# Turning x of one chunk by a transfer on ScalarE's queue, and a new order in six passes of a fused attention and max-FFN kernel

## The chip, the core and the metric

One core of one Trainium2 chip. Five engines work side by side, each with its own stream of instructions: TensorE (PE, with weight loads shown apart as PEld), VectorE (DVE), ScalarE (ACT), GpSimd (POOL) and SyncE (SP), which here only starts transfers. Transfers started by SP, ACT or POOL stand in that engine's queue and are carried out by the core's 16 DMA engines. The metric is the device time of one execution in microseconds (us), the median of several runs.

## What is computed

A sliding-window attention with sink positions, then a feed-forward layer whose hidden value is the maximum of three products. Batch 4, 8 heads, 768 positions, head size 64; a position sees the first 4 positions and the 128 up to itself.

```python
scores = scale * np.matmul(q, k.transpose(0, 1, 3, 2))
keep = is_sink | in_window              # pos < 4, or 0 <= rel < 128
scores = np.where(keep, scores, -1000000000.0)
a = softmax(scores)                     # over the last axis
attn = np.matmul(a, v)                  # (4, 8, 768, 64)
x = attn.transpose(0, 2, 1, 3).reshape(3072, 512)
h = np.maximum(np.maximum(x @ w1, x @ w2), x @ w3)   # 512 -> 768
return (h @ w_out).astype(np.float32)                # 768 -> 512
```

## The kernel before, in words

The 3072 positions are cut into 12 chunks of 256 (`NCH = 12`, three per batch entry, `CPB = 3`). For one chunk the steps are:

- `load(ci)` (L90, SP's queue): k, q and v of the chunk, 512 KB each, into raw tiles; two raw tiles of each kind exist. `cast(ci)` (L101, L105, POOL in the loop) makes bf16 of them.
- `turn_dma(ci, 'k')` and `turn_dma(ci, 'q')` (L159 in two halves, L154): transposing transfers on SP's queue that write kT and qT, of which a ring of four exists. The first chunks are turned by TensorE instead.
- `sink_score` (L300) and `score(ci, pairs)` (L274): TensorE, 64 rows of the array per head, two heads to a pair, four pairs; a pair's scores fill two PSUM banks. A chunk that opens a batch entry has no sink step, and its scores have three blocks instead of four. `sink_k` and `sink_v` (L230, L316) prepare the sinks of a batch entry, once for each.
- `expo` (L286, ACT; L306 for the sinks), which frees the two banks of a pair, and `mask` (L292, DVE).
- `av_open` (four banks, and the sink products L332, 32 rows of the array each) and `av(ci, pair)` (L350 on TensorE, then L355 and L358 on DVE, which write a pair's part of x).
- x turned into xT: `xpose(ci, t)` does it on TensorE (L371, four matmuls against an identity for each half, then a copy out of PSUM, L372), `xpose_dma(ci)` by one transposing transfer on SP's queue (L377). Chunks 0 to 3 use `xpose`, chunks 4 to 11 `xpose_dma`. Three xT tiles exist.
- `ffn_h(ci, fp, wi)` (L390): eight matmuls of the chunk's xT with 256 columns of weight matrix `wi`; with `wi = 0` ACT copies the result to h (L397), with 1 or 2 DVE takes the maximum (L401). Nine calls make the chunk's h.
- `ffn_y(ci, t)` (L411): six matmuls of 512 columns, then a copy out of PSUM (L413), and `store(ci)` (L427, SP's queue).

The order is written out by hand: every engine carries out its instructions in the order in which the calls stand. PSUM's eight banks are given out by a list: `bank` takes the one at its front, and the step that empties a bank puts it at the back, so the order of the calls decides which bank each step takes and whose end it waits for. Chunks 0 to 2 and the attention of chunk 3 stand in a long straight part; then a loop runs over `i = 3 .. 11`. A pass of the loop has, interleaved, the loads of chunk `i + 3`, the casts and turns of chunk `i + 2`, the attention of chunk `n = i + 1`, the first layer of chunk `i` and the second layer of chunk `m = i - 1`.

In a pass before, SP's queue gets the three loads, k in two halves, q, the store of `m` and x of `n`, in this order. TensorE gets the sink scores, pairs 0 and 1, `ffn_y(m, 0)`, pairs 2 and 3, `ffn_y(m, 1)`, two `ffn_h`, and then the four `av` between further `ffn_h`. Both copies of y are on DVE.

Of the kernel before, what the change touches and what calls it, by code (L numbers as in the profile page):

```python
# [16 lines left out]
def kernel(  # L17
# [31 lines left out]
    with tc.manual_schedule():  # L49
# [26 lines left out]
        def load(ci, what="kqv", gate=None, part=None, parts=1):  # L76
            if ci >= NCH:
                return
            b, c = divmod(ci, CPB)
            t0 = c * 256  # L80
            for w in what:
                src = {"k": k, "q": q, "v": v}[w]
                if (ci, w) not in raws:
                    raws[ci, w] = raw.tile([128, H, 2, D], F32, tag=w + "_raw", name=w + "_raw")
                dst = raws[ci, w]
                if gate is not None:
                    gate(dst[0:1, 0, 0, 0:1])
                n = H // parts
                for g in range(parts) if part is None else (part,):
                    nc.sync.dma_start(  # L90
                        out=dst[:, n * g:n * g + n],
                        in_=src[b, n * g:n * g + n, t0:t0 + 256]
                            .rearrange("h (p i) d -> p h (i d)", i=2))
# [56 lines left out]
        def turn_dma(ci, w):  # L150
            if ci >= NCH:
                return
            if w == "q":
                nc.sync.dma_start_transpose(  # L154
                    out=qT[ci % RING].rearrange("q p i n r -> q (p i) (n r)"),
                    in_=bfs[ci, w].rearrange("s p i a d -> s (p i a d)"))
                return
            for n in range(2):
                nc.sync.dma_start_transpose(  # L159
                    out=kT[ci % RING][:, n].rearrange("q p i r -> q (p i) r"),  # L160
                    in_=bfs[ci, w][64 * n:64 * n + 64].rearrange("q p i a d -> q (p i a d)"))
# [64 lines left out]
        def sink_k(b):  # L226
            x = kT[(b * CPB) % RING]
            for a in range(2):
                hp = slice(64 * a, 64 * a + 64)
                nc.gpsimd.tensor_copy(  # L230
                    ks[b % 2][hp, :, 4 * a:4 * a + 4].rearrange("q p (r i) -> q p r i", i=2),
                    x[hp, 0, :, :, 0:2].rearrange("q p i r -> q p r i"))
# [77 lines left out]
        def sink_v(b):  # L310

            x = vb[(b * CPB) % RING]
            sv = bank([128, 2, D + 1], F32, "sv")
            for a in range(2):
                for p in range(NP):
                    nc.tensor.matmul(  # L316
                        sv[32 * p:32 * p + 32, a], lhsT=sel[:, a], rhs=x[:, 0, 2 * p + a],
                        start=True, stop=True, tile_position=(0, 32 * p))
            nc.vector.tensor_copy(vs[b % 2], sv)
            give(sv)  # L320
# [18 lines left out]
        def av(ci, p):  # L339
            b, c = divmod(ci, CPB)  # L340
            o = os_[ci, p]
            e = es[ci, p][0]
            first = c == 0
            for t in range(2):
                for a in range(2):
                    blocks = [(1, ci, 0)] if t == 0 else [(2, ci, 0), (3, ci, 1)]
                    if t == 0 and c:
                        blocks = [(0, ci - 1, 1)] + blocks
                    for s, cv, n in blocks:
                        nc.tensor.matmul(  # L350
                            o[:, t, a], lhsT=e[:, a, s], rhs=vb[cv % RING][:, n, 2 * p + a],
                            start=first, stop=True, skip_group_check=True)
                        first = False
            rc = work.tile([128, 2, 2], F32, tag="rc", bufs=4, name="rc")
            nc.vector.reciprocal(rc, o[:, :, :, D])  # L355
            if p == 0:
                xs[ci] = work.tile([128, 2, NP, 2, D], BF16, tag="x", bufs=2, name="x_sb")
            nc.vector.tensor_mul(xs[ci][:, :, p], o[:, :, :, 0:D],  # L358
                                 rc.unsqueeze(3).to_broadcast([128, 2, 2, D]))
            give(o)  # L360
# [3 lines left out]
        def xpose(ci, t, eng=None):  # L364
            eng = eng or nc.scalar
            if t == 0:
                xTs[ci] = work.tile([128, 2, DS, 128], BF16, tag="xT", bufs=3, name="xT")
            pt = bank([128, DS, 128], BF16, "xt")
            x = xs[ci][:, t].rearrange("q p a d -> q (p a d)")
            for ds in range(DS):  # L370
                nc.tensor.transpose(pt[:, ds], x[:, ds * 128:(ds + 1) * 128], ident)  # L371
            (nc.scalar.copy if eng is nc.scalar else eng.tensor_copy)(xTs[ci][:, t], pt)  # L372
            give(pt)

        def xpose_dma(ci):
            xTs[ci] = work.tile([128, 2, DS, 128], BF16, tag="xT", bufs=3, name="xT")
            nc.sync.dma_start_transpose(  # L377
                out=xTs[ci].rearrange("q t s r -> q (t s) r"),
                in_=xs[ci].rearrange("q t p a d -> q (t p a d)"))

# [2 lines left out]
        def ffn_h(ci, fp, wi, cuts=1):  # L383
            if ci not in hs:
                hs[ci] = work.tile([128, FB, 256], BF16, tag="h", bufs=3, name="h_sb")
            hp = bank([128, 2, 256], F32, "h_ps")
            for f in range(2):
                c0 = (2 * fp + f) * 128
                for ds in range(DS):
                    nc.tensor.matmul(  # L390
                        hp[:, f].rearrange("q (i t r) -> q i t r", i=2, t=2),
                        lhsT=w_sb[wi][:, ds, c0:c0 + 128],
                        rhs=xTs[ci][:, :, ds].rearrange("q t (i r) -> q i t r", i=2),
                        start=(ds == 0), stop=(ds == DS - 1))
            dst = hs[ci][:, 2 * fp:2 * fp + 2]
            if wi == 0:
                nc.scalar.copy(dst, hp)  # L397
            else:
                for f in range(cuts):
                    x = slice(2 * f // cuts, 2 * (f + 1) // cuts)  # L400
                    nc.vector.tensor_max(dst[:, x], dst[:, x], hp[:, x])  # L401
            give(hp)
# [40 lines left out]
        def cast(ci, q=None):  # L443
            if ci >= NCH:
                return
            for w in "kq":
                for g in range(2):
                    cast_qk(ci, w, g, q if q and w == "q" else nc.gpsimd)
            for n in range(2):
                for i in range(2):  # L450
                    cast_v(ci, n, i, nc.gpsimd)
# [195 lines left out]
        ffn_h(2, 2, 2)  # L647
        av(3, 3)
        av(3, 2)
        ffn_h(2, 1, 1)  # L650
        ffn_h(2, 1, 2)
        load(5, 'v', gate=after(0))
        xpose(3, 0, nc.scalar)
        xpose(3, 1, nc.vector)
        ffn_h(2, 2, 1)
        for i in range(3, NCH):
            n, m = i + 1, i - 1
            more = n < NCH
            if more:
                n % CPB == 1 and (sink_k(n // CPB), sink_v(n // CPB))  # L660
            load(i + 3)
            cast(i + 2)
            turn_dma(i + 2, 'k')
            turn_dma(i + 2, 'q')
            if more:
                sink_score(n)
            if more:
                score(n, (0, 1))
            if more:
                expo(n, 0)  # L670
            if more:
                expo(n, 1)
            ffn_y(m, 0, nc.vector)
            if more:
                score(n, (2, 3))
            if more:
                mask(n, 0)
            if more:
                mask(n, 1)
            if more:  # L680
                expo(n, 2)
            ffn_y(m, 1, nc.vector)
            store(m)
            if more:
                mask(n, 2)
            if more:
                expo(n, 3)
            ffn_h(i, 0, 0)
            if more:
                mask(n, 3)  # L690
            ffn_h(i, 0, 1)
            if more:
                av_open(n); av(n, 0)
            ffn_h(i, 0, 2)
            if more:
                av(n, 1)
            ffn_h(i, 1, 0)
            if more:
                av(n, 2)
            ffn_h(i, 1, 1)  # L700
            if more:
                av(n, 3); xpose_dma(n)
            ffn_h(i, 1, 2)
            ffn_h(i, 2, 0)
            ffn_h(i, 2, 1)
            ffn_h(i, 2, 2, 1 if i + 2 < NCH else 2)

        ffn_y(NCH - 1, 0, nc.vector)
        store_half(NCH - 1, 0)
# [40 lines left out]
```

## Time and profile before

| | |
|---|---|
| median of 3 runs | 180.19 us (180.06 to 180.62) |
| profiled execution | 180.04 us, of it span 178.3 us |
| granted TensorE clock | 1.00 |
| busy | PE 170.4 us, DVE 129.2, ACT 81.4, POOL 64.6 |
| DMA | 34.90 MB, mean 196 GB/s |

Times inside the profile count from the start of its span. A row of a group of instructions names the line of the kernel, the engine, the operation and the tile written, then the tiles read; a wait is put down to what ended last before the instruction. The chain that ended last is followed back from the end of the program: each piece is what released the next. For a transfer the profile has the time in which its issuing engine is held and the time until its data have landed.

### The profile page before, as it was taken

What the parts mean: (1) busy time and instruction counts of PE and PEld (TensorE: products, weight loads), DVE (VectorE), ACT (ScalarE), POOL (GpSimd) and SP (SyncE); (2) the same over time, 40 slices, a digit from 0 to 9 for tenths busy, and PEclk for the clock granted to TensorE, in tenths of its full rate; (3) what the DMA queues carried; (4) which work ended last, traced back from release to release, by engine and by line L of the source; (5) the groups of instructions that cost most, each with busy time, mean ns of one, the idle gap of its engine ahead of it and who ended that gap; (6) DMA issues with size and microseconds to landing.
All of it is one profiled execution on the core that took longest, in us unless ns stands there. A gap on an engine that the chain in (4) does not pass through costs nothing.

```text
span 178.3 us, 4662 instructions
## 1 busy us (share of the span) xinstructions
PE 170.4 (96%) x1873; PEld 126.3 (71%) x1873; DVE 129.2 (72%) x277; ACT 81.4 (46%) x163; POOL 64.6 (36%) x121
## 2 busy tenths in 40 slices
PE   7689999999999999999999999999999999999991
PEld 2445889766687587587696696696795795796870
DVE  3189752799799796696794994994975975976451
ACT  3386734863962922912715715615426426420210
POOL 4478620323663793282280670670550000000000
PEclk9999999999999999999999999999999999999999
DMA  5999999999999997995996996996978707202203
GB/s 147 290 286 209 243 212 249 214 288 290 332 184 258 295 170 184 256 279 129 293 282 136 299 210 152 296 215 155 285 211 136 162 0 64 119 6 56 118 0 118
DMA packets 69029, 34.90 MB, mean 196 GB/s; under 512 B 26512, under 2 KB 67472, under 8 KB 69008
## 3 DMA queue, kind: packets, MB, share of 16 engines
q1 hardware_dynamic: 64912, 31.33, 78.1%
q0 software_dynamic: 3952, 3.15, 11.3%
q8 instruction: 14, 0.23, 0.5%
q10 hardware_dynamic: 144, 0.13, 0.2%
q14 instruction: 7, 0.06, 0.1%
HBM read 25.17 MB, written 6.29 MB: 176 GB/s over the span
## 4 chain that ended last, share of the span: by engine, by line
PE 79%; DMA 13%; POOL 2%; ACT 2%; issue 1%; DVE 1%; POOLq 0%; ACTq 0%
PE h_ps L390 47%; PE y_ps L411 18%; DMA q_raw<-in_q_dram 9%; PE o L350 6%; PE st L274 5%; DMA w<-in_moe_w_dram 5%; PE o L332 1%; POOL w L239 1%; PE y_ps L421 1%; ACT q_bf L101 1%; PE sk L300 1%; PE xt L371 1%; ACT kT L144 1%; PE pt L115 1%; DVE h_sb L401 0%
## 5 line engine op out<-in xcount | busy, mean ns | idle before, releaser
L390 PE MATMUL h_ps<-xT,w 128*128 128x256 bf16 x864 | 103.8, 273 | 0.2 <-DVE h_sb L401 0.2
L390 PEld LDWEIGHTS <-w 128*128 128x128 bf16 x864 | 81.3, 98 | 11.7 <-issue 0.6
L401 DVE TENSOR_TENSOR h_sb<-h_sb,h_ps 128x512 bf16<-128x512 bf16 (+1 forms) x74 | 49.1, 669 | 17.5 <-PE h_ps L390 14.9
L397 ACT CAST h_sb<-h_ps 128x512 bf16<-128x512 f32 x36 | 21.1, 587 | 59.5 <-PE h_ps L390 59.4
L286 ACT ACTIVATE e_sb<-st 128x512 bf16<-128x512 f32 (+1 forms) x96 | 45.7, 573 | 5.1 <-PE st L274 5.0
L411 PE MATMUL y_ps<-wo,h_sb 128*128 128x512 bf16 x138 | 33.6, 380 | 0.0
L105 POOL CAST vb<-v_raw 64x512 bf16<-64x512 f32 x40 | 25.9, 648 | 19.8 <-DMA v_raw<-in_v_dram 18.2
L292 DVE TENSOR_TENSOR e_sb<-e_sb,msk 128x1024 bf16<-128x1024 bf16 (+1 forms) x42 | 30.0, 748 | 1.1 <-ACT e_sb L286 1.0
L101 POOL CAST k_bf<-k_raw 128x512 bf16<-128x512 f32 x17 | 12.8, 772 | 41.4 <-DMA k_raw<-in_k_dram 39.9
L413 DVE COPY y_sb<-y_ps 128x512 f32<-128x512 f32 x19 | 13.1, 691 | 13.0 <-PE y_ps L411 12.7
L411 PEld LDWEIGHTS <-h_sb 128*128 128x128 bf16 x138 | 11.9, 98 | 14.0 <-issue 2.5
L358 DVE TENSOR_TENSOR x_sb<-o,rc 128x256 bf16<-128x256 f32 x48 | 20.4, 424 | 1.7
L350 PE MATMUL o<-vb,e_sb 128*128 128x65 bf16 x352 | 18.3, 194 | 0.3 <-DVE vb L105 0.2
L350 PEld LDWEIGHTS <-e_sb 128*128 128x128 bf16 x352 | 16.0, 98 | 2.6 <-DVE vb L105 0.4
L274 PE MATMUL st<-qT,kT 64*128 64x128 bf16 (+1 forms) x256 | 14.3, 238 | 0.6 <-DVE qT L141 0.6
L274 PEld LDWEIGHTS <-kT 64*128 64x128 bf16 x256 | 8.2, 94 | 7.9 <-issue 6.2
L101 POOL CAST q_bf<-q_raw 128x512 bf16<-128x512 f32 x17 | 12.3, 742 | 4.1 <-DMA q_raw<-in_q_dram 3.7
L355 DVE RECIPROCAL rc<-o 128x4 f32<-128x4 f32 x48 | 8.4, 175 | 1.2 <-PE o L350 0.9
L306 ACT ACTIVATE e_sink<-sk 128x256 bf16<-128x256 f32 x8 | 3.1, 384 | 8.9 <-PE sk L300 8.9
L177 PE MATMUL warm<-wz 128*128 128x512 bf16 x15 | 5.2, 507 | 1.2 <-DVE wz L166 1.2
L101 DVE CAST q_bf<-q_raw 128x512 bf16<-128x512 f32 x5 | 2.1, 422 | 4.5 <-DMA q_raw<-in_q_dram 4.5
L239 POOL DMA_DIRECT2D w<-in_moe_w_dram x6 | 4.9, 810 | 0.1
(70 smaller groups left out, 69.8 us busy)
## 6 DMA issues: line engine op xcount, KB each, us to landing
k_raw<-in_k_dram SPq DMA_DIRECT2D x12, 512.0 KB, 5.0
q_raw<-in_q_dram SPq DMA_DIRECT2D x12, 512.0 KB, 6.1
v_raw<-in_v_dram SPq DMA_DIRECT2D x12, 512.0 KB, 7.1
out_dram<-y_sb SPq DMA_DIRECT2D x11, 512.0 KB, 3.7
w<-in_moe_w_dram POOLq DMA_DIRECT2D x4, 256.0 KB, 9.1
w<-in_moe_w_dram POOLq DMA_DIRECT2D x1, 768.0 KB, 8.3
wo<-in_moe_w_out_dram POOLq DMA_DIRECT2D x1, 768.0 KB, 10.7
w<-in_moe_w_dram POOLq DMA_DIRECT2D x1, 512.0 KB, 9.4
```

What stands on the lines that cost most here:

```text
L101: f(x[:, 2 * g:2 * g + 2].rearrange("q p i a d -> q p a i d"), y[:, 4 * g:4 * g + 4].rearrange("q (p a) i d -> q p a i d", a=2))
L105: eng.tensor_copy(vb[ci % RING][64 * i:64 * i + 64, n, :, 0:D], raws[ci, "v"][64 * n:64 * n + 64, :, i])
L274: nc.tensor.matmul(st[a][:, s:s + q1 - q0].rearrange("q n (i r) -> q n i r", i=2), lhsT=x[hp, n, p].rearrange("q i r -> q (i r)"), rhs=qc[ ...
L286: nc.scalar.activation(e[:, a, lo:], st[a][:, lo:], AF.Exp, scale=scale)
L292: (eng or nc.vector).tensor_mul(e[:, :, lo:], e[:, :, lo:], msk0 if lo else msk)
L350: nc.tensor.matmul(o[:, t, a], lhsT=e[:, a, s], rhs=vb[cv % RING][:, n, 2 * p + a], start=first, stop=True, skip_group_check=True)
L358: nc.vector.tensor_mul(xs[ci][:, :, p], o[:, :, :, 0:D], rc.unsqueeze(3).to_broadcast([128, 2, 2, D]))
L390: nc.tensor.matmul(hp[:, f].rearrange("q (i t r) -> q i t r", i=2, t=2), lhsT=w_sb[wi][:, ds, c0:c0 + 128], rhs=xTs[ci][:, :, ds].rearrang ...
L397: nc.scalar.copy(dst, hp)
L401: nc.vector.tensor_max(dst[:, x], dst[:, x], hp[:, x])
L411: nc.tensor.matmul(yp, lhsT=hs[ci][:, fb, t * 128:(t + 1) * 128], rhs=wo[:, fb], start=(fb == 0), stop=(fb == FB - 1))
L413: (nc.scalar.copy if eng is None else eng.tensor_copy)(ys[ci][:, t], yp)
```

## The change

x of chunk 3 is no longer turned by TensorE. `xpose_dma` gets a parameter for the engine whose queue it uses, and chunk 3's x is turned by one transposing transfer that ScalarE issues. It stands where the attention of chunk 3 ends, before the last three `ffn_h` of chunk 2. In the built program the instruction on ScalarE waits for x and for the three earlier transposing transfers on SP's queue (q and k of chunk 4); the next transposing transfer on SP's queue (k of chunk 5) waits for its landing.

The passes `i = 4` to `9` get a new order; `i = 3`, `10` and `11` keep the old one. In the new order the scores of pairs 0, 3 and 1 stand in a row, then both blocks of `ffn_y(m)`, then pair 2, `av_open` and the first `av`; `ffn_h(i, 1, 0)` is the first of chunk `i`, and the nine `ffn_h` stand in another order. The copy of `ffn_y(m, 1)` is on ScalarE. On SP's queue q of chunk `i + 2` comes first, then the three loads, k, x of `n`, and the store of `m` last.

```diff
-        def xpose_dma(ci):
+        def xpose_dma(ci, eng=None):
             xTs[ci] = work.tile([128, 2, DS, 128], BF16, tag="xT", bufs=3, name="xT")
-            nc.sync.dma_start_transpose(
+            (eng or nc.sync).dma_start_transpose(
                 out=xTs[ci].rearrange("q t s r -> q (t s) r"),
                 in_=xs[ci].rearrange("q t p a d -> q (t p a d)"))
...
         av(3, 3)
         av(3, 2)
+        xpose_dma(3, nc.scalar)
         ffn_h(2, 1, 1)
         ffn_h(2, 1, 2)
         load(5, 'v', gate=after(0))
-        xpose(3, 0, nc.scalar)
-        xpose(3, 1, nc.vector)
         ffn_h(2, 2, 1)
         for i in range(3, NCH):
...
+            if i == 3 or i >= NCH - 2:
...
+            else:
+                if more:
+                    n % CPB == 1 and (sink_k(n // CPB), sink_v(n // CPB))
+                if more:
+                    sink_score(n)
+                cast(i + 2)
+                turn_dma(i + 2, 'q')
...
+                    score(n, (0,))
+                    expo(n, 0)
+                    score(n, (3,))
+                    score(n, (1,))
+                    expo(n, 1)
+                    expo(n, 3)
+                ffn_y(m, 0, nc.vector)
+                    mask(n, 0)
+                ffn_y(m, 1)
+                    score(n, (2,))
+                    mask(n, 3)
+                    av_open(n)
+                    mask(n, 1)
+                    expo(n, 2)
+                    av(n, 0)
+                    mask(n, 2)
+                load(i + 3)
+                ffn_h(i, 1, 0)
+                ffn_h(i, 0, 0)
+                    av(n, 1)
+                ffn_h(i, 1, 2)
+                ffn_h(i, 0, 1)
+                    av(n, 2)
+                turn_dma(i + 2, 'k')
+                    av(n, 3)
+                ffn_h(i, 1, 1)
+                ffn_h(i, 2, 0)
+                ffn_h(i, 0, 2)
+                ffn_h(i, 2, 1)
+                    xpose_dma(n)
+                ffn_h(i, 2, 2, 1 if i + 2 < NCH else 2)
+                store(m)
```

Where a call in the new branch is indented further, it stands under `if more:`, which holds in all six passes.

More of the change, by code (lines that the diff above doesn't have):

```diff
@@ L658 @@
             more = n < NCH
[L659 to L706, printed above, removed]
+            if i == 3 or i >= NCH - 2:
[7 more added lines that the diff above has]
+                    sink_score(n)
+                if more:
+                    score(n, (0, 1))
+                if more:
+                    expo(n, 0)
+                if more:
+                    expo(n, 1)
+                ffn_y(m, 0, nc.vector)
+                if more:
+                    score(n, (2, 3))
+                if more:
+                    mask(n, 0)
+                if more:
+                    mask(n, 1)
+                if more:
+                    expo(n, 2)
+                ffn_y(m, 1, nc.vector)
+                store(m)
+                if more:
+                    mask(n, 2)
+                if more:
+                    expo(n, 3)
+                ffn_h(i, 0, 0)
+                if more:
+                    mask(n, 3)
+                ffn_h(i, 0, 1)
+                if more:
+                    av_open(n); av(n, 0)
+                ffn_h(i, 0, 2)
+                if more:
+                    av(n, 1)
+                ffn_h(i, 1, 0)
+                if more:
+                    av(n, 2)
+                ffn_h(i, 1, 1)
+                if more:
+                    av(n, 3); xpose_dma(n)
+                ffn_h(i, 1, 2)
[3 more added lines that the diff above has]
+            else:
+                if more:
+                    n % CPB == 1 and (sink_k(n // CPB), sink_v(n // CPB))
+                if more:
+                    sink_score(n)
+                cast(i + 2)
+                turn_dma(i + 2, 'q')
+                if more:
+                    score(n, (0,))
+                if more:
+                    expo(n, 0)
+                if more:
+                    score(n, (3,))
+                if more:
+                    score(n, (1,))
+                if more:
+                    expo(n, 1)
+                if more:
+                    expo(n, 3)
+                ffn_y(m, 0, nc.vector)
+                if more:
+                    mask(n, 0)
+                ffn_y(m, 1)
+                if more:
+                    score(n, (2,))
+                if more:
+                    mask(n, 3)
+                if more:
+                    av_open(n)
+                if more:
+                    mask(n, 1)
+                if more:
+                    expo(n, 2)
+                if more:
+                    av(n, 0)
+                if more:
+                    mask(n, 2)
+                load(i + 3)
+                ffn_h(i, 1, 0)
+                ffn_h(i, 0, 0)
+                if more:
+                    av(n, 1)
+                ffn_h(i, 1, 2)
+                ffn_h(i, 0, 1)
+                if more:
+                    av(n, 2)
+                turn_dma(i + 2, 'k')
+                if more:
+                    av(n, 3)
+                ffn_h(i, 1, 1)
+                ffn_h(i, 2, 0)
+                ffn_h(i, 0, 2)
+                ffn_h(i, 2, 1)
+                if more:
+                    xpose_dma(n)
+                ffn_h(i, 2, 2, 1 if i + 2 < NCH else 2)
+                store(m)
```

## The prediction

> **What bounds the kernel now.** I read the page's busy shares first, then the chain that ended last, then the loop pass by pass (an answer by windows, cut where the chain shows a pass begin), and then the queues round the start of the loop.
>
> ```profile
> PE 170.4 (96%) x1873; PEld 126.3 (71%) x1873; DVE 129.2 (72%) x277; ACT 81.4 (46%) x163; POOL 64.6 (36%) x121
> PE 79%; DMA 13%; POOL 2%; ACT 2%; issue 1%; DVE 1%; POOLq 0%; ACTq 0%
> 70.42:83.70 13.28, 13.28 (x154) 9.90 (x156) 10.19 (x20) 6.09 (x12) 5.95 (x10) 1.00 0.93 222
> 83.70:95.97 12.27, 12.27 (x132) 9.32 (x136) 9.46 (x20) 5.04 (x11) 4.98 (x8) 1.00 0.98 236
> ```
>
> The window rows give length, then busy time of PE, PEld, DVE, ACT and POOL, then the granted clock. In a pass of the loop PE is busy for the whole pass, at clock 1.00, while DVE has 3 us to spare and ACT 7. So from the loop's start to the end the time is the sum of PE's work. A change gains only what it takes off PE, and every wait that it puts on PE is paid in full. The 0.15 us between the profiled execution (180.04) and the median (180.19) I leave as it is: terms come from the profile and are taken off the median.
>
> **Part 1: x of chunk 3.** The chain in order of time (start, us) around the eight TensorE transposes:
>
> ```profile
> 55.55 0.11 PE xt L371 x2
> 55.66 0.03 issue
> 55.69 0.51 PE xt L371 x6
> ...
> 59.86 1.40 PE y_ps L411 x6
> 61.26 1.75 PE h_ps L390 x16
> ```
>
> They go: 0.11 + 0.03 + 0.51 = 0.65 us off PE, on the path. Their two PSUM banks and the two copies to xT (ACT and DVE) go too, neither on the path. All that follows reaches PE 0.65 earlier, so the first reader of xT(3), `ffn_h(3,0,0)`, stands at 61.26 - 0.65 = 60.61. That is the deadline of the new transfer. When can it start, and what does such a transfer take?
>
> ```profile
> 55.21 0.42 DVE L358 TENSOR_TENSOR x_sb<-o,rc 128x256 bf16<-128x256 f32 x1
> L377 SPq DMA_TRANSPOSE xT<-x_sb x8: 1237/1237/1881, 68.1 to 159.2; - x8
> DMA to landing us min/median/max: 3.0/3.2/4.9
> L154 SPq DMA_TRANSPOSE qT<-q_bf x8: 1259/1270/4330, 45.8 to 136.6; - x8
> DMA to landing us min/median/max: 3.2/4.2/7.3
> ```
>
> x(3) is complete at 55.63; I take the issue at 55.70. ScalarE's transfer also waits for the three transposes of chunk 4 on SP's queue; the last two (SP's rows below) are issued by 53.05 and land 3.1 after their issue began, so before that. Undisturbed it lands at 55.70 + 3.0 = 58.7, two us early. The worst transfer of the same size (qT, 7.3) gives 63.0, which is 2.4 late. What else the DMA engines do decides between these ends. SP's queue at that time, with the landing of kT from the DMA view of 45 to 54 us and of qT from that of 63 to 70:
>
> ```profile
> kT<-k_bf SPq DMA_TRANSPOSE x2, 3.1
> ...
> qT<-q_bf SPq DMA_TRANSPOSE x1, 3.2
> ...
> 50.22 2.83 SPq L159 DMA_TRANSPOSE kT<-k_bf  x2
> 53.77 0.39 SPq L90 DMA_DIRECT2D v_raw<-in_v_dram  x1
> 54.21 1.11 SPq L90 DMA_DIRECT2D k_raw<-in_k_dram  x1
> 55.38 1.65 SPq L90 DMA_DIRECT2D q_raw<-in_q_dram  x1
> 57.12 1.52 SPq L90 DMA_DIRECT2D v_raw<-in_v_dram  x1
> 58.75 5.44 SPq L159 DMA_TRANSPOSE kT<-k_bf  x2
> 64.28 1.26 SPq L154 DMA_TRANSPOSE qT<-q_bf  x1
> ...
> 76.99 1.27 SPq L154 DMA_TRANSPOSE qT<-q_bf  x1
> ```
>
> Four loads of 512 KB are under way. The DMA view, first of 158.8 to 163 us, where one transfer of x runs alone, then of 56 to 63, where loads run, then of 23 to 28, where weights on POOL's queue and loads on SP's run together (packets, MB, share of 16 engines):
>
> ```profile
> q1 hardware_dynamic: 1056, 0.26, 32.7%
> ```
> ```profile
> q1 hardware_dynamic: 4009, 2.02, 112.8%
> ```
> ```profile
> q0 software_dynamic: 1209, 0.60, 87.6%
> q1 hardware_dynamic: 905, 0.46, 43.1%
> ```
>
> A transpose packet takes 4.2 x 16 x 0.327 / 1056 = 21 ns, a load packet 7 x 16 x 1.128 / 4009 = 31 ns, and two queues move about packet for packet. The transfer has 66 packets per engine: alone 66 x 21 ns = 1.4 us, alternating with loads 66 x 52 = 3.4. Landing then takes 3.0 + 2.0 = 5.0 to 5.1, at 60.8: late by 0.2. I take +0.2 (bounds 0 and +2.4).
>
> The Trainium skill, "DMA: Bandwidth & Descriptors", section "Issuing engines are not separate DMA queues", speaks against this step: transfers started from different engines run on the same 16 DMA engines and interleave, and a second issuing engine saves only issue time. By that rule the new queue buys no bandwidth and the transfer shares with the loads, which gives the +0.2; a reader who trusts the 3.0 of the undisturbed row would have 0. The rows of 23 to 28 us agree with the rule for POOL and SP; no row of before has ScalarE's queue beside SP's.
>
> ScalarE itself is held while it issues: 1.24 (SP's shortest) to 4.33 (its longest, behind its own queue's loads). ScalarE's queue is empty, so I take 1.24: held from 55.70 to 56.94. Behind it stand the exponentials of chunk 4:
>
> ```profile
> 57.41 0.38 ACT L306 ACTIVATE e_sink<-sk 128x256 bf16<-128x256 f32 x1 [0.81 <-PE sk L300]
> 57.72 4.03 ACT L286 ACTIVATE e_sb<-st 128x512 bf16<-128x512 f32 x8
> ```
>
> They start at 56.94 instead of some 0.2 earlier. The first PE instruction that needs a bank from them is `ffn_y(2,1)`, which takes the second bank of pair 0, free at about 56.94 + 0.31 + 2 x 0.50 + 0.1 = 58.4, and stands at 59.86 - 0.65 = 59.21. Cover 0.8; cost 0. With 4.33 it would be 60.03 and PE would wait 2.3.
>
> On SP, `turn_dma(5,'k')` now also waits for the new transfer to land: 60.8 instead of 58.75, with k's second half, q of chunk 5, `store(2)` and x of chunk 4 behind it. q landed at 64.28 + 3.2 = 67.5 and is needed by the sink scores at 70.42 - 0.65 = 69.77. A delay of 2.05 makes it 69.5: cover 0.2, cost 0. If the loads push it further it costs that much: bounds 0 and +0.7.
>
> **Part 2: the order of six passes** (i = 4 to 9; i = 3, 10, 11 keep theirs). No PE instruction is added or removed, but switches between kinds of matmul cost PE time. Rows of the chain:
>
> ```profile
> 70.64 0.55 PE st L274 x12
> 71.19 1.40 PE y_ps L411 x6
> 72.59 0.55 PE st L274 x12
> ...
> 76.29 0.22 PE o L332 x8
> 76.51 0.35 PE o L350 x8
> 77.73 0.24 PE o L350 x8
> 161.49 2.59 PE y_ps L411 x12
> ```
>
> Six y matmuls take 2.59 / 2 = 1.295 by themselves and 1.40 behind scores (64 rows of the array): 0.105 for that switch. Full-array `o` behind the 32-row sink products (L332) takes 0.35 against 0.24: the same 0.11. Before, a pass with sinks has three switches to the full array (scores to y twice, sinks to o); after, scores of pairs 0, 3, 1 lead to both y blocks, and pair 2's scores to the sinks and o: two. Runs of scores stay two. So 0.105 off each pass with sinks: n = 5, 7, 8, 10, four of the six: 0.42. In the two passes without sinks the second switch moves from y to `o`: 0.
>
> New waits in these passes, counted from a pass's start with these durations. Scores of three pairs end at about 1.0 and hold six banks; y(m,0) takes the bank of the last `ffn_h`, whose maximum on DVE is done at +0.72 (below: to 71.14 where the pass starts at 70.42). Cover 0.3, 0.1 where `sink_v` also stands there.
>
> ```profile
> 69.65 1.49 DVE L401 TENSOR_TENSOR h_sb<-h_sb,h_ps 128x512 bf16<-128x512 bf16 x2 [1.03 <-PE h_ps L390]
> 72.63 0.69 DVE L413 COPY y_sb<-y_ps 128x512 f32<-128x512 f32 x1 [1.49 <-PE y_ps L411]
> 73.24 1.28 DVE L292 TENSOR_TENSOR e_sb<-e_sb,msk 128x1024 bf16<-128x1024 bf16 x2
> ```
>
> The first `av` now stands behind both y blocks and pair 2: 1.3 + 0.33 + 0.22 = 1.85 after y(m,0) ends. Its mask is done 0.61 + 0.64 + 0.1 = 1.35 after it: cover 0.5. ScalarE takes the copy of y(m,1) (0.59) from DVE, before pair 2's exponentials; pair 2's banks and mask are next needed 2.5 us later. `xpose_dma(n)` is issued at about +10, lands by +15 at 4.9, and is first read by `ffn_h(i,1,0)` at 13.2 + 4.6 = +17.8: cover 2.8. On SP, q of chunk i+2 now goes ahead of the three loads and k behind them; the last of this chain was issued at 76.99 (SP's rows) and at the median of 4.2 landed at 81.2, 2.5 before its pass at 83.70; the same transfers in another order put the last in the same place, one issue (1.3) later at most. POOL's casts run ahead of PE in either order. Cost 0; bounds 0 and, where the thinnest covers fail by 0.3 each, 6 x 0.3 = +1.8.
>
> Sum: 180.19 - 0.65 - 0.42 + 0.2 = 179.3.
>
> **Rivals.**
> A, slower: x of chunk 3 lands late. One place, `ffn_h(3,0,0)` at 60.61; from 6.0 us of landing on (55.70 + 6.0 = 61.7) the 1.07 saved is eaten. For it: 7.3 for qT beside loads, and chunk 5's k, 5.44 in issue. Against: both stood behind loads of their own queue. At 7.3: 180.19 - 1.07 + 2.4 = 181.5; ScalarE held for 4.33 gives nearly the same (2.3) and overlaps with it.
> B: banks bind in the new passes. For: three pairs, sinks and y use all eight banks in the first us. Against: DVE's 3 us of room. Even at +0.15 per pass: 179.3 + 0.9 = 180.2, no change; at the bound 181.1.
> C: the reordering saves nothing, since PE had no gap and the switch only moves (it also leads from scores to sinks): 179.3 + 0.42 = 179.7.
>
> **How the numbers follow.** A difference under 0.3% (0.54 us) can't be told from none. Forecast, 178.9 to 179.6: 0.50. A: 0.22, of it 0.17 slower and 0.05 within. B: 0.15, of it 0.10 slower and 0.05 within. C: 0.07, split evenly between faster and within. Late chunk-5 turns and what I have not seen: 0.06, 0.04 slower. Together faster 0.54, same 0.15, slower 0.31. The range reaches from all of the saving with no wait and a little more (178.8) into A (181.4); forecast alone 178.9 to 179.6.
>
> **What would show it.** Right: no xt in the chain near 55.6, PE without a gap before the h products of chunk 3, the transfer on ScalarE's queue landing in about 5, y blocks back to back in six passes (12 matmuls in 2.7), and passes with sinks of 13.17 instead of 13.28. Wrong: a wait of h_ps for DMA xT near 60.6, of st for a DVE or ACT bank at pass starts, of sk for qT near 69.8, or a ScalarE issue well over 1.24.

## The result, and the profile after

The changed kernel takes 184.84 us (median of 6 runs, 183.21 to 185.86) against 180.23 for the kernel before in the same comparison: ratio 1.0256, 95% interval 1.0229 to 1.0284. It is 4.6 us slower where 0.9 us less was forecast, and lies outside the range. The profiled execution took 185.41 us, span 183.6.

The chain that ended last around the start of the loop in the changed kernel (start, length, what):

```profile
55.80 1.76 PE h_ps L390 x16
57.56 0.10 DVE h_sb L401
57.66 7.45 DMA xT<-x_sb
...
65.16 3.34 PE h_ps L390 x16
...
76.06 0.22 PE sk L300 x4
76.28 0.77 PE st L274 x18
77.05 2.69 PE y_ps L411 x12
```

The chain no longer runs through TensorE. It leaves it for the transfer of x of chunk 3 and returns 7.5 us later to the first h products of chunk 3: the wait named for rival A, at its place. The waits for that transfer, from the answer by tile for xT on ScalarE's queue:

```profile
L377 ACTq DMA_TRANSPOSE xT<-x_sb x1: 1337/1337/1337, 57.7 to 57.7; - x1
  PEld L390: 3.0, 1
  PE h_ps L390: 2.6, 1
```

ScalarE itself is held for only 1.34 us. The matmuls wait 2.6 us.

The windows of the changed kernel (PE, PEld, DVE, ACT, POOL busy, then the granted clock, DMA share, GB/s) show a second loss:

```profile
10.00:15.00 5.00, 4.90 (x53) 2.43 (x50) 4.07 (x11) 3.68 (x9) 3.63 (x7) 0.66 1.21 264
...
60.00:65.00 5.00, 2.60 (x22) 0.98 (x19) 4.31 (x6) 3.35 (x7) 3.84 (x5) 1.00 1.28 180
65.00:70.00 5.00, 4.84 (x43) 3.41 (x44) 1.57 (x4) 0.58 (x1) 3.62 (x6) 0.66 1.16 260
```

After a stretch in which PE was idle for 2.4 of 5 us, the granted clock is 0.66 in the next 5 us, and the 16 h products take 3.34 us instead of 1.75. The clock is also 0.66 at 10 to 15 us, ahead of everything that the change touches, where the profile of the kernel before has none; the same kernel measured again (`e8_after_again`, below) did not show that dip, so it belongs to this execution and not to the change.

Profile against profile the 5.37 us (185.41 - 180.04) come apart like this. By the end of `ffn_h(2, 1, 2)` the changed kernel is 2.01 late (57.56 against 55.55): the early dip, and PE that was idle for 1.0 in the stretch from 35 to 45. Nothing ahead of that point was changed. From there to the first h of chunk 3 it takes 7.60 us instead of 5.71: +1.89, which is the wait less the 0.65 of transposes that are gone. The 16 products add 1.59 for the clock. That is 5.49; the remaining -0.12 is what follows, above all the later passes:

```profile
76.06:89.23 13.17, 13.17 (x154) 10.00 (x156) 9.82 (x19) 6.75 (x13) 5.17 (x10) 1.00 0.85 197
...
101.50:114.84 13.34, 13.34 (x164) 10.06 (x164) 9.49 (x20) 6.68 (x13) 4.78 (x8) 1.00 1.12 227
114.84:128.01 13.17, 13.17 (x154) 10.00 (x156) 9.31 (x19) 6.68 (x13) 4.78 (x8) 1.00 1.09 221
```

The rows are those of the passes n = 5, 7 and 8. In the kernel before the pass n = 5 took 13.28, and n = 7 and 8:

```profile
95.97:109.31 13.34, 13.34 (x164) 9.97 (x164) 10.54 (x21) 6.09 (x12) 5.93 (x8) 1.00 1.06 220
109.31:122.60 13.29, 13.29 (x155) 9.92 (x156) 10.34 (x20) 6.09 (x12) 6.34 (x10) 1.00 1.07 218
```

The passes n = 5 and 8 win 0.11 and 0.12. The pass n = 7, where `sink_v` stands in front, wins nothing; nor does n = 6, which has no sinks (12.27 in both).

The six runs, with the mean granted clock of each:

```
clock    1.000    .988    .987    .981    .981    .978
us      183.21  184.24  184.28  185.41  185.86  185.50
```

The run with no loss of clock is 3.0 us above the kernel before; those with a lower clock are another 1.0 to 2.65 above it. These need not be the clock's alone: only one of the six was profiled, and the wait for the transfer differs between executions (2.6 here, 4.6 in `e8_after_again`).

### The profile page after: what moved, and what is told of

It reads as the page before. It is cut to its first block, busy times and chain, and to the rows that moved or that the text cites. A ratio compares the mean times of both kernels' runs of the same rounds, so it can differ in the third digit from the quotient of the medians.

```text
span 183.6 us, 4632 instructions
## 1 busy us (share of the span) xinstructions
PE 172.4 (94%) x1865; PEld 127.0 (69%) x1865; DVE 126.6 (69%) x270; ACT 84.2 (46%) x168; POOL 61.1 (33%) x121
## 4 chain that ended last, share of the span: by engine, by line
PE 85%; DMA 7%; DVE 4%; ACT 1%; issue 1%; POOL 0%; POOLq 0%; DVEq 0%; ACTq 0%
PE h_ps L390 51%; PE y_ps L411 15%; PE o L350 7%; PE st L274 6%; DMA xT<-x_sb 4%; DMA q_raw<-in_q_dram 3%; DVE e_sb L292 2%; PE pt L115 1%; PE o L332 1%; PE pt L137 1%; ACT kT L144 1%; PE warm L177 1%; PE y_ps L421 1%; PE xt L371 1%; PE sk L300 1%
## 5 line engine op out<-in xcount | busy, mean ns | idle before, releaser
L390 PEld LDWEIGHTS <-w 128*128 128x128 bf16 x864 | 82.3, 99 | 13.7 <-DMA xT<-x_sb 3.0
L411 PE MATMUL y_ps<-wo,h_sb 128*128 128x512 bf16 x138 | 32.7, 380 | 1.0 <-DVE h_sb L401 1.0
L292 DVE TENSOR_TENSOR e_sb<-e_sb,msk 128x1024 bf16<-128x1024 bf16 (+1 forms) x42 | 29.2, 726 | 1.3 <-ACT e_sb L286 1.1
L101 POOL CAST k_bf<-k_raw 128x512 bf16<-128x512 f32 x17 | 10.8, 658 | 45.7 <-issue 28.3
L413 DVE COPY y_sb<-y_ps 128x512 f32<-128x512 f32 x13 | 9.0, 690 | 13.5 <-PE y_ps L411 13.4
L350 PE MATMUL o<-vb,e_sb 128*128 128x65 bf16 x352 | 17.5, 195 | 0.3 <-DVE e_sb L292 0.3
L350 PEld LDWEIGHTS <-e_sb 128*128 128x128 bf16 x352 | 15.2, 99 | 2.7 <-issue 0.5
L101 POOL CAST q_bf<-q_raw 128x512 bf16<-128x512 f32 x17 | 10.1, 617 | 4.7 <-DMA q_raw<-in_q_dram 4.7
L413 ACT COPY y_sb<-y_ps 128x512 f32<-128x512 f32 x10 | 5.9, 586 | 7.5 <-PE y_ps L411 7.4
L101 DVE CAST q_bf<-q_raw 128x512 bf16<-128x512 f32 x5 | 2.9, 571 | 3.6 <-DMA q_raw<-in_q_dram 3.6
```

The lines of the kernel that those rows point to most:

```text
L101: f(x[:, 2 * g:2 * g + 2].rearrange("q p i a d -> q p a i d"), y[:, 4 * g:4 * g + 4].rearrange("q (p a) i d -> q p a i d", a=2))
L292: (eng or nc.vector).tensor_mul(e[:, :, lo:], e[:, :, lo:], msk0 if lo else msk)
L350: nc.tensor.matmul(o[:, t, a], lhsT=e[:, a, s], rhs=vb[cv % RING][:, n, 2 * p + a], start=first, stop=True, skip_group_check=True)
L390: nc.tensor.matmul(hp[:, f].rearrange("q (i t r) -> q i t r", i=2, t=2), lhsT=w_sb[wi][:, ds, c0:c0 + 128], rhs=xTs[ci][:, :, ds].rearrang ...
L411: nc.tensor.matmul(yp, lhsT=hs[ci][:, fb, t * 128:(t + 1) * 128], rhs=wo[:, fb], start=(fb == 0), stop=(fb == FB - 1))
L413: (nc.scalar.copy if eng is None else eng.tensor_copy)(ys[ci][:, t], yp)
```

## The experiments

### Each part alone

`e1_part1` is the kernel before with chunk 3's x on ScalarE's queue and the old order of the passes; `e2_part2` has the new passes and lets TensorE turn x as before. `e10_part2_again` measures the latter a second time.

```diff
 e1_part1, against the kernel before
+        xpose_dma(3, nc.scalar)
         ffn_h(2, 1, 1)
         ffn_h(2, 1, 2)
         load(5, 'v', gate=after(0))
-        xpose(3, 0, nc.scalar)
-        xpose(3, 1, nc.vector)
```

> Only part 1 of the change: x of chunk 3 turned by the transfer on ScalarE's queue, all passes in the old order. Theory L (the transfer lands late, because SP's four loads are served first or together with it): all of the loss is here; PE waits for xT before the h products of chunk 3 by 2 to 3 us, and the run is at 182 to 186 us, by how much the granted clock drops after the wait. Rival P (the new passes cost): this run is at 179.5 to 180, near 180.2 - 0.65.

> Only part 2: the six passes in the new order, chunk 3 turned by TensorE as before. Theory L: nothing is lost here; the passes with sinks are 0.11 shorter but for the two that also have sink_v, where a wait for a bank takes it back, so 180.2 - 0.2 = 180.0. Rival P: 182 or more, with waits of PE for banks in the passes. The clock should stay at 1.00 by L; a drop in the first 15 us here too would show that the drop there has nothing to do with part 1.

> The new passes alone once more, x of chunk 3 turned by TensorE as before. If the gain of the four passes with sinks is real (2 x 0.11 without and 2 x 0 with `sink_v` give 0.2 to 0.3), the ratio to the kernel before comes out at 0.998 to 0.999; if the first measurement was chance, at 1.000.

`e1_part1` takes 184.88 us (median of 4, 182.97 to 187.65). Two of the four kept a clock of 1.000, 182.97 and 183.45, and the ratio is made from these: 1.0167, 1.0126 to 1.0208. The chain and the wait of the execution of 182.97:

```profile
56.23 7.75 DMA xT<-x_sb
...
64.02 1.92 PE h_ps L390 x16
```
```profile
PE h_ps L390 <- DMA xT<-x_sb: 2.7, 1, 2.7
```

This execution kept its clock, and the loss is 2.76 by the first h of chunk 3 (64.02 against 61.26) and 0.17 in its 16 products: 2.93 in all, which is 182.97 - 180.04. So all of the loss is there by the end of these products. The wait of 2.68, less the 0.65 of transposes, makes 2.03 of the 2.76. The other 0.73 lies ahead of the transfer, in `ffn_h(2, 1, 1)`, whose products begin at 54.37 here and, by the same view of PE in order of time, at 53.64 in the kernel before; nothing was changed up to there, so it is a difference between two executions.

`e2_part2` gives 179.97 against 180.34, ratio 0.9979 (0.996 to 0.9998); the second time 180.05 against 180.12, 0.9994 (0.9977 to 1.0012). The profile of `e2_part2` lists no wait of PE at the starts of the new passes. Its passes n = 5 and 7, by windows:

```profile
70.33:83.50 13.17, 13.17 (x155) 9.99 (x156) 9.31 (x19) 6.68 (x13) 5.17 (x10) 1.00 0.93 206
...
95.77:109.11 13.34, 13.34 (x165) 10.10 (x164) 9.48 (x20) 6.69 (x13) 4.45 (x8) 1.00 1.21 239
```

The new order is worth 0.11 in a pass with sinks and nothing where `sink_v` stands in front: about 0.22 in all. That agrees with both ratios, but it is less than the 0.54 us that a measurement can tell from nothing.

### The same transfer on SP's queue

```diff
 e3_sp_queue, against the changed kernel
-        xpose_dma(3, nc.scalar)
+        xpose_dma(3)
```

> The changed kernel with the transfer of x of chunk 3 on SP's queue at the same place of the program, so that v of chunk 5 and the loads of chunk 6 stand behind it. Theory L: it lands 3.0 to 3.2 after x is complete, PE has no wait, and the run is at 180.2 - 0.65 - 0.2 = 179.3. Rival T (a transposing transfer beside this much work of PE and DVE is slow at this place, whatever the queue): a landing of 5 us or more and 181 or more.

180.66 us (10 runs), ratio 1.0026 (1.0006 to 1.0046). On SP's queue the transfer stands in front of the four loads instead of beside them. Issued at 56.00, it landed after 5.0 us, not the 3.0 to 3.2 that were expected, and PE hardly waited. The answer by tile for the nine transfers of x on SP's queue, and the DMA view from 55 to 57 us:

```profile
L377 SPq DMA_TRANSPOSE xT<-x_sb x9: 1232/1239/2257, 56.0 to 160.0; - x9
  PEld L390: 0.5, 1
```
```profile
xT<-x_sb SPq DMA_TRANSPOSE x1, 5.0
```

The 2.6 us at h are gone, but not all of the gain is left. The loads now start later, chunk 5's k and q are turned behind them, and the sink scores of chunk 5 wait. From the chain:

```profile
66.55 4.81 DMA qT<-q_bf
...
71.40 0.29 PE sk L300 x4
```

They begin at 71.40 instead of 70.42 before. The place of the transfer decides, and one queue over, it takes the time from another transfer.

### How many loads stand in front

The DMA view of the changed kernel from 57.7 us, just behind the issue on ScalarE's queue (57.66), to 61.2, and then the next 1 us; q1 is SP's queue, q10 ScalarE's (packets, MB, share of 16 engines):

```profile
q1 hardware_dynamic: 1909, 0.97, 102.1%
```
```profile
q10 hardware_dynamic: 500, 0.13, 112.5%
q1 hardware_dynamic: 185, 0.09, 36.4%
...
```

For 3.5 us after its issue the transposing transfer does not move one packet. In that time SP's queue moves 0.97 MB, nearly all of two loads of 512 KB (1024 packets each): v of chunk 5 and k of chunk 6, whose issue had ended by 57.13. The issue of a third, q of chunk 6, had begun at 57.18, ahead of ScalarE's too, but it ended only at 59.11, and its packets came behind the transfer. Then the picture turns round, and the loads stand. If the transfer waits for the loads that are fully issued before it, the wait must shrink with their number. Three kernels try it. In `e4_late_loads` the last v load of chunk 5 and the loads of chunk 6 move behind the turns of chunk 5. In `e5_gate_all` the four loads wait until xT of chunk 3 has landed (a small copy on POOL reads it and writes into the raw tile); in `e6_gate_six` only the three of chunk 6 do. `e8_after_again` is the changed kernel without an edit.

```diff
 e4_late_loads, against the changed kernel, in pass i = 3
-        load(5, 'v', gate=after(0))           # and load(6) of the pass
...
+        for w in "kq":
+            for g in range(2):
+                cast_qk(5, w, g, nc.gpsimd)
+        turn_dma(5, 'k'); turn_dma(5, 'q')
+        load(5, 'v', gate=after(0)); load(6)
...

 e5_gate_all, against the changed kernel
+        def xt_gate(dst):
+            nc.gpsimd.tensor_copy(dst, xTs[3][0:1, 0, 0, 0:1])
-        load(5, 'v', gate=after(0))           # ahead of pass i = 3
+        cast_part(5, 'kq')                    # in pass i = 3
+        load(5, 'v', gate=xt_gate); load(6)
+        cast_part(5, 'v')
+        turn_dma(5, 'k'); turn_dma(5, 'q')

 e6_gate_six, against the changed kernel (its v load of chunk 5 stays)
+        cast_part(5, 'kq')                    # in pass i = 3
+        load(6, 'k', gate=xt_gate); load(6, 'qv')
+        cast_part(5, 'v')
+        turn_dma(5, 'k'); turn_dma(5, 'q')
```

> The changed kernel, ScalarE's queue kept, with the load of v of chunk 5 and the three loads of chunk 6 moved behind the turns of chunk 5 on SP's queue, so that no load is in flight beside the transfer. Theory L: it lands in 3.0 to 3.3, PE has no wait there, 179.3 us, if the later loads are still in time. Rival Q (ScalarE's queue is slow by itself): a landing above 6 as in the changed kernel, PE waits 2 us or more, 182 or more.

> The changed kernel with all four loads (v of chunk 5, k, q and v of chunk 6) held until x of chunk 3 has been turned. ScalarE's transfer then has no load beside it. Theory O (the two queues are served in the order in which transfers were started, so it waited for the loads started before it): first packets about 1.1 after the issue, landing 3.0 to 3.3, no wait of PE before the h products of chunk 3. Rival Q (ScalarE's queue is slow by itself): landing above 6. The turns of chunk 5 come behind the held loads, so a later wait of PE for q of chunk 5, 1 to 3 us, is expected by both, and the time says little.

> As the run before, but only the loads of chunk 6 are held; v of chunk 5 is started before the transfer as in the changed kernel. Theory O: the transfer's first packets come when the 1024 packets of that one load have been served, 0.5 to 1.5 later than with no load; landing 3.5 to 5. Rival S (packets of both queues alternate, as forecast): first packets at 1.1 after the issue while load packets still run. Rival Q: above 6.

> The changed kernel itself, to see which of its losses return: the wait for xT of 2.5 to 3 us in every execution; the drop of the granted clock behind it in some; and the drop in the first 15 us with its 1 to 2 us, which lies ahead of all that was changed, in some or none. By the runs at clock 1.00 the wait alone gives 183.0 to 183.4; with drops up to 186.

Times: `e4_late_loads` 189.17 us (4 runs, ratio 1.0488, 1.0454 to 1.0521), `e5_gate_all` 184.88 and `e6_gate_six` 184.79 (one run each), `e8_after_again` 185.67 (4 runs, ratio 1.0269, 1.0206 to 1.0331). From the packets of the same traces: how many load packets moved ahead of the transfer's first, and when that first packet moved and the transfer landed, in us from the issue on ScalarE:

```
                  loads whose issue had   load packets
kernel            ended    begun          ahead          first packet   landing
e5_gate_all         0        0                0              1.3          4.8
e6_gate_six         1        1              814              2.7          6.4
changed kernel      2        3             1905              3.6          7.5
e1_part1            2        3             1954              4.0          7.7
e8_after_again      2        3             1829              3.3          9.5
e4_late_loads       2        3             1814              3.3          8.2
```

The DMA view of `e6_gate_six` from 55.5 to 58.1 us, the wait before its first packet, has only the rest of a store and most of the one load:

```profile
q1 hardware_dynamic: 867, 0.61, 94.5%
```

The landing of 3.5 to 5 expected for `e6_gate_six` came to 6.4. The wait grows with the loads in front, and it is nearly their whole time: the first packet moved when 94 to 234 packets of them were left. An even share from the start, as forecast, is refuted. That a transfer on ScalarE's queue is slow by itself is refuted by the 1.3 us of `e5_gate_all`, where 55.8 to 57.0 has no packet of any queue. The order is not strict, however: in `e4_late_loads` the third load and the transfer ran side by side once the first two were through. Its DMA view from 65.5 to 68.5 us:

```profile
q1 hardware_dynamic: 683, 0.35, 68.9%
q10 hardware_dynamic: 880, 0.23, 58.6%
```

Whether the order is kept in the DMA engines or already where the packets are made is not told apart by these runs.

The landings hold a second cost that does not follow the loads. With none in front `e5_gate_all` still took 4.8 us and not the 3.0 to 3.3 expected, so the rival named for `e3_sp_queue`, that a transposing transfer is slow at this place on any queue, is half right: 4.8 and 5.0 on the two queues against 3.0 in the quiet row. The rest, up to 7.5, comes with the loads in front. In the changed kernel the transfer's last packets crawl from 62.2 to 64:

```profile
DMA  8000059999999000000000000010010101000000
GB/s 34 17 17 17 17 108 273 267 267 262 284 193 11 0 0 0 0 0 0 0 0 0 0 0 0 0 11 6 6 11 6 11 6 11 11 6 11 11 6 11
...
q10 hardware_dynamic: 333, 0.09, 136.2%
```

All 16 engines are nearly still for over 1 us, with packets of the transfer counted as under way (the share of 136%). It begins at 62.7, while one engine fetches 16 KB of instructions, a single packet from 62.0 to 63.4; in `e5_gate_all` a standstill from 58.1 to 59.9 begins during the same fetch (57.8, 1.35 us). But the fetch is not shown to be the cause. In the kernel before, the transposing transfer of k of chunk 5 stood in the same way from 63.6 to 65.5 with no fetch between 61.2 and 68.5. The DMA view of the kernel before from 63.5 to 65 us has one queue alone, at few packets and a high share:

```profile
q1 hardware_dynamic: 241, 0.07, 185.5%
```

What makes a transposing transfer stand stays open.

In these two kernels, taking the loads away from the front does not pay, since they have to come somewhere. The waits of `e5_gate_all` and then of `e6_gate_six`:

```profile
PE sk L300 <- DMA qT<-q_bf: 3.8, 1, 3.8
```
```profile
PE sk L300 <- DMA qT<-q_bf: 2.4, 1, 2.4
PE h_ps L390 <- DMA xT<-x_sb: 1.2, 1, 1.2
```

What h no longer waits for, the sink scores of chunk 5 wait for. `e4_late_loads` missed its question: in that build ScalarE's transfer came to wait for SP's transposes of chunk 5 and was issued only at 61.81, when three moved loads had been begun, two of them fully issued. What it shows is the price of a ScalarE queue that stands: scores for which the exponentials had not freed banks, and 8.2 us of landing.

```profile
PE st L274 <- ACT e_sink L306: 4.4, 1, 4.4
PE h_ps L390 <- DMA xT<-x_sb: 2.7, 1, 2.7
```

`e8_after_again` repeats the loss, with no early dip: the first h products of the profile begin at 18.41 against 18.33 before. Its wait was longer than the 2.5 to 3 expected, and the clock fell further:

```profile
PE h_ps L390 <- DMA xT<-x_sb: 4.6, 1, 4.6
```
```profile
60.00:65.00 5.00, 0.78 (x4) 0.17 (x2) 3.39 (x5) 1.54 (x4) 4.26 (x5) 0.89 1.23 156
65.00:70.00 5.00, 4.63 (x34) 3.04 (x35) 0.81 (x2) 0.59 (x1) 3.38 (x6) 0.50 0.88 170
70.00:75.00 5.00, 5.00 (x62) 4.37 (x61) 3.73 (x11) 0.59 (x1) 0.25 (x1) 0.93 0.41 133
```

### Turns before loads

`e7_sp_turn_first` takes the SP queue of `e3_sp_queue` and puts the turns of chunk 5 ahead of all four loads, so that neither x of chunk 3 nor chunk 5's k and q stand behind a load.

```diff
 e7_sp_turn_first, against the changed kernel
-        xpose_dma(3, nc.scalar)
+        xpose_dma(3)
-        load(5, 'v', gate=after(0))           # ahead of pass i = 3
+        cast_part(5, 'kq')                    # in pass i = 3
+        turn_dma(5, 'k'); turn_dma(5, 'q')
+        load(5, 'v', gate=after(0)); load(6)
+        cast_part(5, 'v')
```

> The changed kernel with x of chunk 3 on SP's queue, behind it k and q of chunk 5, and only then the four loads. Theory O: x lands in 3.0 to 3.2, q of chunk 5 lands before 64, PE waits for neither; 180.3 - 0.65 - 0.3 = 179.3 to 179.4. Rival: the loads of chunk 6, some 6 us later, make the turns of chunk 6 late and PE waits in the pass of i = 5: 180 or more.

180.38 us (13 runs), ratio 1.0006 (0.9982 to 1.0029): equal to the kernel before, and not better than the new passes alone, though eight transposes are off TensorE. The profiled execution was the slowest of the 13 (182.49), so it shows where the order is vulnerable and not the median. In it x of chunk 3 landed 5.4 us after its issue, and h waited 0.7 for it. Later in its chain:

```profile
66.22 8.54 DMA v_raw<-in_v_dram
...
81.04 5.21 DMA kT<-k_bf
```

The late loads push the next chunk's turn. In each of the places tried, what one transfer more took off PE went into another wait.

### The bank of `sink_v`

```diff
 e9_sink_v_early, against e2_part2
-                    n % CPB == 1 and (sink_k(n // CPB), sink_v(n // CPB))
+                    n % CPB == 1 and sink_k(n // CPB)
...
+                if n + 1 in (7, 10):
+                    sink_v((n + 1) // CPB)
                 ffn_h(i, 2, 2, 1 if i + 2 < NCH else 2)
```

> The new passes alone, with `sink_v` of the entries 2 and 3 moved out of the starts of passes n = 7 and 10 to stand ahead of the last `ffn_h` of the passes in front (n = 6 and 9). Theory: in these two passes the bank that `sink_v` takes is the one for which the third pair's scores wait (0.87 for 18 score products instead of 0.77). Then the scores take 0.77 in all four passes with sinks, and the time is 2 x 0.1 under the new passes alone. Rival: the wait has another cause, or `sink_v`, whose 32 columns now stand between two blocks of h, costs a switch of array form (0.105) in each of its new places; then the time is that of the new passes alone.

180.17 us (12 runs), ratio 0.9999 (0.998 to 1.0017). The chain of `e2_part2` at the start of pass n = 7, and then that of `e9_sink_v_early`:

```profile
95.77 0.18 PE sv L316 x8
95.95 0.11 PE sk L300 x4
96.06 0.87 PE st L274 x18
```
```profile
95.38 0.18 PE sv L316 x8
95.55 0.98 PE h_ps L390 x8
96.53 0.22 PE sk L300 x4
96.76 0.77 PE st L274 x18
```

Both sides were right. With `sink_v` away the scores take 0.77, so its bank was what they waited for: in `e2_part2` DVE's cast of `sv`, which frees that bank, ended at 96.70, and by 0.77 for 18 products the third pair's would have begun at about 96.6 (an estimate). But its 32 columns now stand between two blocks of full width: the eight h products behind them take 0.98 instead of 0.87, and the sink scores 0.22 instead of 0.11. The piece costs 1.28 + 0.87 for the same work as 1.16 + 0.87 before: 0.12 more.

No version beats the kernel before by more than the measurement can tell. The nearest is `e2_part2`.

## Why the prediction was wrong, point by point

**x of chunk 3: the step that failed is the landing of 5.0 to 5.1 (the +0.2).** It took the 3.0 of a quiet transfer and added 2.0, because it let the transposing transfer alternate packet for packet with the loads, a ratio taken from POOL's and SP's queues at 23 to 28 us. Both terms were too small. ScalarE's and SP's queues did not share in that way: the transfer waited 3.3 to 4.0 us for the two loads that were fully issued, where its first packet came after 1.3 with none in front. And with none in front it landed after 4.8, not 3.0. Measured: 7.45, and a wait of 2.6 where 0.2 was forecast.

The Trainium skill, "DMA: Bandwidth & Descriptors", section "Issuing engines are not separate DMA queues", says that transfers from different engines interleave on the same 16 DMA engines. The same engines, yes; but in the 3.5 us of the DMA view above nothing interleaved, and here the measurement decides. Behind the loads in front the two queues did run side by side in `e4_late_loads`. That a second issuing engine saves issue time alone, its other half, nothing here speaks against.

With the 7.5 measured the sum would have been 55.70 + 7.5 = 63.2 against the deadline of 60.61, a wait of 2.6. That was rival A's size (2.4, from the 7.3 of qT), and "both stood behind loads of their own queue" was the wrong reason to discount it: loads of another queue count as well.

**The clock was not in the sum.** It was 1.00 throughout the trace of before, where PE never stood for long in the loop, and the price of a wait on PE was put at its length. A wait of 2.6 brought half the clock for 3.41 us in the profiled execution, 1.59 us on the 16 products behind it, and a wait of 2.7 brought none in `e1_part1`.

The two do not make the whole way. With a wait of 2.6 and half of part 2 the forecast would have been about 181.9; the run without a loss of clock took 183.21, and it was not profiled. In `e1_part1` such a remainder was 0.73 ahead of the transfer and 0.17 in the products behind it. What it was in the run of 183.21 stays open.

**ScalarE's issue, 1.24 taken:** 1.34 measured, with no bank late. Right.

**The turns of chunk 5, cover 0.2, cost 0 (bounds 0 and +0.7):** where xT no longer made h late, this cover failed: the sink scores waited 1.0 for qT in `e3_sp_queue`. The place was right and the bound of +0.7 too small. In `e10_part2_again`, where this part of the queue is the kernel before's, they too ended a chain through that landing (70.65), so the cover was thin without part 1.

**0.65 off PE:** gone from the chain, and eaten by the wait.

**Part 2, -0.42:** the mechanism was right in the passes n = 5 and 8 (13.17 forecast, 13.17 measured). In the passes with `sink_v`, where the cover was called 0.1, the scores waited 0.1 (0.87) and the saving went into that: by the passes about -0.22 instead of -0.42. Rival C (nothing saved) is wrong by the passes and can't be told from the total; rival B came out at its thinnest place only.

## What to carry to other kernels

Before moving work from TensorE to a transfer, list every load that is fully issued ahead of it, on the other engine's queue too, and add what they still have to move; a queue of its own was no way past them here. In a stretch where the DMA engines are nearly full, one transfer more can make another one late, so the work removed from TensorE has to be set against the first wait that this brings. And a wait of 2 or 3 us on a TensorE that is otherwise never idle should be priced with a possible stretch at half clock behind it.

## What the runs showed of the hardware that was not expected

- Loads fully issued on SP's queue went ahead of a transposing transfer on ScalarE's: first packets 1.3, 2.7 and 3.3 to 4.0 us after the issue with 0, 1 and 2 loads of 512 KB in front. A third load, whose issue had begun but not ended, did not go ahead; it came behind or ran side by side with the transfer.
- Transposing transfers nearly stood still for 1.5 to 1.9 us on all engines at once: in the changed kernel and `e5_gate_all` while a 16 KB instruction fetch was under way, in the kernel before with no fetch near.
- The clock is lost in fixed pieces. The clock records of the traces have half the clock for 3.41 us in the changed kernel (twice, from 10.9 and from 65.5) and for 6.83, twice as much, in `e8_after_again`. The window rows agree: 0.66 over 5 us is 1.7 us of work lost, that is 3.4 us at half rate; the 0.89, 0.50 and 0.93 of `e8_after_again` lose 0.55 + 2.5 + 0.35 = 3.4. The Trainium skill, "TensorE: Matmul & The Clock Gate", Part 1, gives a window of about 3.4 us: after an idle one the clock goes to half. The size agrees; a wholly idle window was not needed here. Count each trace in steps of 3.41 us from its first clock record. In the step ahead of a fall to half clock behind a wait in the loop, PE was idle for 2.56 in the changed kernel, 3.09 in `e8_after_again`, 2.54 in `e5_gate_all` and 2.33 in `e6_gate_six`. The wait of 2.7 in `e1_part1` fell on two steps, 1.74 and 0.94, and the clock stayed. So whether a wait of this size cost clock seems to have hung on where it fell, and that was chance. It is read from these traces and no run tried it; nor do they give a sure limit, since the early loss of the changed kernel followed a step with 1.78 idle.
